# The fifth chunk's output rows transposed as float32r from a copy, and its gating and routing issued two to three products later

## The chip, the cores and the metric

The kernel runs on one core of one Trainium2 chip. A time is the device time of one execution in microseconds. The kernel before takes 934.78 us (median of three runs, 934.42 to 935.09).

## The reference

Three stages follow each other. A linear attention over 4 batches, 8 heads, 576 positions and 64 channels gives 2304 rows of 512. A dense layer takes the elementwise maximum of three products and multiplies it with a fourth matrix. A mixture of 8 experts sends every row to the two experts with the largest noisy gate values.

```python
x = attn_out.transpose(0, 2, 1, 3).reshape(B * S, H * D)          # 2304 x 512
h = np.maximum(np.maximum(x @ w1, x @ w2), x @ w3)                # 2304 x 768
x = h @ w_out                                                     # 2304 x 512
logits = x @ w_gate
noise_scale = np.log1p(np.exp(x @ w_noise))
noisy_logits = logits + noise_scale * noise                       # 2304 x 8
top2 = np.argpartition(-noisy_logits, 2, axis=1)[:, :2]
top2_w = softmax of the two chosen values
for e in range(8):                                                # hidden width 1024
    out[rows of e] += top2_w * (np.maximum(x[rows] @ e_w1[e], 0) @ e_w2[e])
```

## The kernel before, in words

Every large product is made of three TensorE products of float32r operands: each operand is split into a high part and the rest, and high times high, high times rest and rest times high are summed in PSUM.

The dense layer works on six chunks of 384 rows (`NCHUNK` is 6, a chunk is three tiles of 128 rows; in the code they are counted from 0, so the fifth chunk is 4 and the last is 5). For a chunk, `first` (L899) is called for six blocks `f` of the hidden width and three weights `j`, 18 times; one call is 12 matmuls and is called a product here, numbered 0 to 17 in a chunk. After the three products of a block, `larger` (L909 on VectorE, L907 on ScalarE), `hidden_high` (L916) and `hidden_low` (L920) make the block's hidden operand, and `second` (L930, 9 matmuls) adds it to the chunk's output in three PSUM banks. The last `second` of a chunk is issued behind product 0 of the next chunk, and `finish` then copies the three output tiles out: `x2_out` (L937 on ScalarE) into the tile `x2`, and a DMA on SP's queue (L942) into the table `x2d` in HBM.

What follows for a chunk `c - 1` is laid between the products of chunk `c`, in four pieces of `tail`: piece 0 transposes two of the three output tiles on TensorE (`x2_turn`, 8 transposes), piece 1 the third (4 transposes), piece 2 computes the gate values (`gates`, L970), piece 3 turns them back to rows (`gates_turn`, L982) and starts the generator `route` by `route_at`. `TAILS` says behind which products the pieces stand: the first tuple for chunks 1 to 4, the second for the last chunk, in which the fifth chunk's rows are handled. For chunks below `PLAIN` the transposes read a second tile, `x2r`, of type float32r, which a DMA on SP's queue (L947) copies from `x2`; there are two such tiles for three copies. For the others the transposes read `x2` as plain float32 (L957).

`route` is a chain of some thirty small instructions on VectorE, with ScalarE and TensorE in between: from the gate values (`lg`, L1003) to the list of slots (`si`, L1073). GpSimd then issues six indirect DMAs (L1077, one per tile and choice), which write each row's number and weight into the table `meta` in HBM, sorted by expert.

The mixture then runs its experts in turn. Expert 0 begins with up to 512 rows (`cap_a`) of the first five chunks; what the last chunk sends to it is handled later as a unit of its own. For it, GpSimd's queue holds, behind the six scatters of the fifth chunk, one DMA that reads the list of rows back from `meta` (`load_meta`, L1106, tile `emeta`) and four indirect DMAs that gather those rows from `x2d` (`gather_x`, L1139, tile `gx`). TensorE transposes the gathered rows (`turn_x`, L1149) behind product 17 of the last chunk: two tiles, then a `second`, then two tiles, then the last `second`. Then come expert 0's products (L1263).

The order on TensorE, ScalarE, VectorE and SP's queue is written out beforehand. Each call is put on a plan at a planned time (`pe` adds a duration to a running clock, `after` adds an offset to it), and the calls are issued in the order of these times. So a change of `TAILS` also shifts the planned times of what is tied to the clock behind it, and the places of those instructions in all four orders. GpSimd's instructions stand in the order in which they are issued.

Between the products stand two more kinds of work. `sum_job` loads quarters of later experts' first weights (L1402, SP), adds them on GpSimd (L1410 to L1415), splits them (L1419 on ScalarE, L1424 on VectorE) and stores both parts (L1426, SP, 512 KB each). In the last chunk `refill` loads expert 0's weights (L1384 and L1381, SP) and splits them (L1434 on ScalarE into `wh`, L1442 on VectorE into `wl`).

Of the kernel before, what the change touches and what calls it, by code (L numbers as in the profile page):

```python
# [38 lines left out]
def tile_linear_attention__then__moe__then__noisy_top2_moe(  # L39
# [37 lines left out]
    NCHUNK = NT // CT  # L77
# [852 lines left out]
                nc.tensor.matmul(st["acc", c][t], a[:, ts_], b_, start=(f == 0 and n == 0),  # L930
                                 stop=(f == F1 - 1 and n == 2))

    PLAIN = NCHUNK - 2

    def x2_out(c, t):
        x2 = pools["m2"].tile([P, DM], F32, name="x2", tag="x2", bufs=3)
# [7 lines left out]
    def x2_copy(c, t):  # L944
        if c < PLAIN:
            x2, st["x2", t] = st["x2", t], pools["m3"].tile([P, DM], F32R, name="x2r", bufs=2)
            dq.dma_start(st["x2", t].bitcast(F32), x2)  # L947

    def x2_turn(c, t):
        x2 = st.pop(("x2", t))  # L950
        pt = bank_t()
        for d in range(KD):
            ds_ = slice(d * P, (d + 1) * P)
            if c < PLAIN:
                nc.tensor.transpose(pt[:, ds_].bitcast(F32R), x2[:, ds_], exact)
# [659 lines left out]
            pe(0.35, gates_turn, c)  # L1615
            route_at(c, clock[0])

    TAILS = (4, 6, 7, 8), (1, 2, 3, 4)
    split_at = [0.0, 0.0]

    pairs = [(e, j) for e in range(E)
# [54 lines left out]
    for c in range(NCHUNK):  # L1676
        if c == NCHUNK - 1:
            split_at.append(clock[0] + 25.0)
        for f in range(F1):
            for j in range(3):  # L1680
# [7 lines left out]

                tails = TAILS[c == NCHUNK - 1]
                if c and 3 * f + j in tails:  # L1690
# [241 lines left out]
```

## Time and profile before

| | before |
|---|---|
| median of 3 runs | 934.78 us (934.42 to 935.09) |
| the profiled execution | 935.69 us |
| its span, first to last instruction | 934.1 us |
| PE busy | 924.6 us (99%) |
| DVE / ACT / POOL busy | 616.9 / 491.6 / 540.7 us |
| mean granted clock of TensorE | 0.998 of full speed |

PE is TensorE's matmul stream, PEld its weight loads, DVE VectorE, ACT ScalarE, POOL GpSimd, SP the SyncE queue that issues most DMAs (SPq, POOLq: instructions that only issue or wait). In a line of the timeline the first number is the start in us from the span's start, the second the duration, then engine, line of the code, operation, the tile written, the tiles read, shapes, and in brackets the idle time before it with what ended it. Consecutive like instructions are merged into one line with their count (x8). Matmuls overlap in the pipeline, so the distance from one start to the next is what one costs.

### The profile page before, as it was taken

To read this page: it belongs to the slowest core of one execution; us is meant where nothing else is said; L and a number is where in the kernel's file an instruction comes from. 1 tells how busy PE (TensorE), PEld (TensorE's weight loads), DVE (VectorE), ACT (ScalarE), POOL (GpSimd) and SP (SyncE) were. 2 spreads that over 40 slices of the span, in tenths; PEclk is the share of its full clock that TensorE was granted. 3 is DMA by queue.
4 is the path that set the end of the run, shared out by engine and by line. 5 is a ranking of instruction groups with operands and counts; after the bars stand their busy time and mean duration, and the time that the engine had idled before them with its cause. 6 is when DMAs were issued, how large, how long until landed. Compare 5 with 4: busy or idle time off the path is not lost. (4 is left out here: it accounts for less than half of the span.)

```text
span 934.1 us, 18533 instructions
## 1 busy us (share of the span) xinstructions
PE 924.6 (99%) x6817; PEld 805.1 (86%) x6817; DVE 616.9 (66%) x1292; ACT 491.6 (53%) x1056; POOL 540.7 (58%) x598
## 2 busy tenths in 40 slices
PE   9999999999999999999999999999999999999997
PEld 7677777799999999999997889798898989898895
DVE  6999999997563737364564367667576767567641
ACT  7999999554333334343445147355463635455340
POOL 6788898645554645646443546465574746455362
PEclk9999999999999999999999999999999999999999
DMA  7676663544757575857575367666575856748212
GB/s 195 171 220 170 185 192 104 193 154 138 227 178 251 181 239 178 248 170 216 164 218 204 91 224 248 242 215 233 174 254 175 285 166 204 264 155 296 94 34 73
DMA packets 131101, 178.07 MB, mean 191 GB/s; under 512 B 35998, under 2 KB 90398, under 8 KB 131010
## 3 DMA queue, kind: packets, MB, share of 16 engines
q1 hardware_dynamic: 119522, 146.94, 49.5%
q0 software_dynamic: 10928, 29.62, 9.5%
q8 instruction: 54, 0.88, 0.4%
q10 hardware_dynamic: 560, 0.33, 0.1%
q14 instruction: 37, 0.30, 0.1%
HBM read 123.05 MB, written 51.24 MB: 187 GB/s over the span
## 5 line engine op out<-in xcount | busy, mean ns | idle before, releaser
L899 PE MATMUL s<-xh,wh 128*128 128x384 f32 x432 | 147.3, 341 | 0.0
L899 PE MATMUL s<-xh,wl 128*128 128x384 f32 x432 | 145.2, 336 | 0.0
L899 PE MATMUL s<-xl,wh 128*128 128x384 f32 x432 | 145.1, 336 | 0.0
L1364 POOL DMA_INDIRECT out_dram<-o,emeta x40 | 47.7, 1191 | 97.6 <-DVE o L1362 30.1
L909 DVE TENSOR_TENSOR a<-s,a 128x384 f32<-128x384 f32 x72 | 40.0, 555 | 88.4 <-PE s L899 87.3
L899 PEld LDWEIGHTS s<-xh,wh 128*128 128x128 f32 x432 | 81.1, 188 | 5.4 <-DVE a L909 2.5
L1354 PE MATMUL p<-wh,hh 128*128 128x512 f32 (+1 forms) x208 | 82.9, 399 | 0.0
L1354 PE MATMUL p<-wh,hl 128*128 128x512 f32 (+1 forms) x208 | 82.5, 396 | 0.2 <-POOL hl L1251 0.2
L899 PEld LDWEIGHTS s<-xl,wh 128*128 128x128 f32 x432 | 81.1, 188 | 1.4
L1354 PE MATMUL p<-wl,hh 128*128 128x512 f32 (+1 forms) x208 | 82.1, 395 | 0.0
L899 PEld LDWEIGHTS s<-xh,wl 128*128 128x128 f32 x432 | 81.1, 188 | 0.0
L1442 DVE TENSOR_TENSOR wl<-raw,wh 128x1024 fp32r<-128x1024 f32 x57 | 69.3, 1221 | 14.8 <-ACT wh L1434 13.8
L1213 PE MATMUL s<-gx,wh 128*128 128x304 f32 x336 | 72.5, 302 | 0.0
L1410 POOL TENSOR_TENSOR raw<-raw 128x256 f32<-128x256 f32 x28 | 24.5, 876 | 74.9 <-DMA raw<-in_moe_w_dram 63.4
L132 DVE TENSOR_TENSOR gx<-t,gx 128x512 fp32r<-128x512 f32 (+3 forms) x88 | 41.0, 480 | 35.7 <-ACT gx L131 32.8
L1434 ACT ACTIVATE wh<-raw 128x1024 fp32r<-128x1024 f32 x57 | 58.9, 1053 | 9.4 <-DMA raw<-in_moe_w_dram 9.4
L245 POOL TENSOR_TENSOR nm<-nm,bits 128x512 int32<-128x512 int32 (+1 forms) x32 | 38.2, 1205 | 40.9 <-DVE nm L235 16.1
L916 ACT ACTIVATE hh<-a 128x384 fp32r<-128x384 f32 x36 | 18.8, 523 | 81.1 <-DVE a L909 76.9
L131 ACT ACTIVATE gx<-t 128x512 fp32r<-128x512 f32 (+3 forms) x88 | 36.5, 437 | 39.3 <-DVE t L1188 30.5
L1213 PEld LDWEIGHTS s<-gx,wh 128*128 128x128 f32 x336 | 55.6, 189 | 0.7
L1077 POOL DMA_INDIRECT meta<-mt,si x36 | 38.8, 1077 | 29.7 <-DVE si L1073 20.5
L1213 PE MATMUL s<-gx,wl 128*128 128x304 f32 x168 | 50.9, 303 | 0.0
(323 smaller groups left out, 2635.0 us busy)
## 6 DMA issues: line engine op xcount, KB each, us to landing
raw<-in_moe_w_dram SPq DMA_DIRECT2D x57, 512.0 KB
raw<-in_moe_w_dram SPq DMA_DIRECT2D x56, 256.0 KB
sums<-qh SPq DMA_DIRECT2D x28, 512.0 KB
sums<-raw SPq DMA_DIRECT2D x28, 512.0 KB
wh<-sums SPq DMA_DIRECT2D x28, 512.0 KB
wl<-sums SPq DMA_DIRECT2D x28, 512.0 KB
bits<-in_moe_w_dram SPq DMA_DIRECT2D x18, 512.0 KB
out_dram<-zrow SPq DMA_DIRECT2D x9, 512.0 KB
```

The costliest lines, as they stand in the source:

```text
L131: nc.scalar.activation(hi, src, AF.Copy)
L132: nc.vector.tensor_tensor(lo, src, hi.bitcast(F32), op=ALU.subtract)
L245: in_order(nc.gpsimd.tensor_tensor(m_[:, i:i + w], m_[:, i:i + w], low[:, i:i + w], op=ALU.add))
L899: nc.tensor.matmul(p_, a[:, d, fs], b_, start=(n == 0), stop=(n == 3 * KD - 1))
L909: nc.vector.tensor_tensor(a, p_, st.pop("a"), op=ALU.max)
L1077: ins = nc.gpsimd.indirect_dma_start(out=meta, out_offset=bass.IndirectOffsetOnAxis(ap=si[:, t, kk:kk + 1], axis=0), in_=mt[:, t, kk, :], ...
L1213: nc.tensor.matmul(bk["p"], a[:, d, fs], b_[:, d, :], start=(d == 0 and i == 0), stop=(d == 1 and i == 2))
L1354: nc.tensor.matmul(p_, a, b_[:, fw], start=(f == 0 and r == 0), stop=(f == (3 if seven(n) else F2 - 1) and r == 2))
L1364: alone(e, nc.gpsimd.indirect_dma_start(out=out, out_offset=bass.IndirectOffsetOnAxis(ap=mt[:m, i, 1:2], axis=0), in_=o[:m], in_offset=Non ...
L1410: ins = nc.gpsimd.tensor_tensor(a22, a21, a22, op=ALU.add)
L1434: nc.scalar.activation(WE[e, i][0], st["w2", e, i], AF.Copy)
L1442: nc.vector.tensor_tensor(wl, st.pop(("w2", e, i)), wh.bitcast(F32), op=ALU.subtract)
```

## The change

`PLAIN` goes from 4 to 5: the fifth chunk's three output tiles are copied into `x2r` by DMA as well, and its 12 transposes become float32r. In the last chunk the four pieces of the fifth chunk's tail move from behind products 1, 2, 3, 4 to behind products 3, 5, 6, 7.

```diff
-    PLAIN = NCHUNK - 2
+    PLAIN = NCHUNK - 1
...
-    TAILS = (4, 6, 7, 8), (1, 2, 3, 4)
+    TAILS = (4, 6, 7, 8), (3, 5, 6, 7)
```

On TensorE's queue, this is where the last chunk's first `second` into its own banks (`p_` with a number, L930) stands before the change: the whole gating is already behind it.

```order
L899 MATMUL s_6164<-xl,wh 128x384
L899 MATMUL s_6164<-xh,wl 128x384
L930 MATMUL p_6181<-wh,hh 128x512
L930 MATMUL p_6181<-wl,hh 128x512
L930 MATMUL p_6181<-wh,hl 128x512
```

And this is the same `second` after the change, on the same queue:

```order
L899 MATMUL s_6147<-xl,wh 128x384
L899 MATMUL s_6147<-xh,wl 128x384
L955 MATMUL t_6166<-exact,x2r 128x128 x4
L930 MATMUL p_6174<-wh,hh 128x512
L930 MATMUL p_6174<-wl,hh 128x512
L930 MATMUL p_6174<-wh,hl 128x512
```

The third tile's transposes (L955, from the copy `x2r`) now stand right ahead of it, and the gates and `gates_turn` come behind it and one and two products on.

On VectorE, in the fifth chunk's route, between the count of the experts' rows (`run`, L1047) and the weights (`den`, L1061), with the rows taken out and put in:

```order
-L1045 TENSOR_TENSOR r_6240<-ohs 128x8
-L1046 TENSOR_TENSOR r_6240<-r_6240,ohs 128x8
-L1047 TENSOR_TENSOR run_96<-r_6240,run_95 128x8
+L1045 TENSOR_TENSOR r_6317<-ohs 128x8
+L1046 TENSOR_TENSOR r_6317<-r_6317,ohs 128x8
+L1047 TENSOR_TENSOR run_96<-r_6317,run_95 128x8
+L1442 TENSOR_TENSOR wl<-raw,wh 128x1024
 L1061 TENSOR_SCALAR den<-ex 128x3
 L1062 RECIPROCAL mt<-den 128x3
 L1063 TENSOR_TENSOR mt<-ex,mt 128x3
```

The first weight split of the refills (L1442), which stood behind the route, now stands within it.

On SP's queue, after the change, the copies stand among the stores of the output tiles, and the third behind two stores of a sum job:

```order
+L947 DMA x2r<-x_6059 128x512
+L942 DMA x2d<-x_6059 128x512
+L947 DMA x2r<-x_6064 128x512
+L942 DMA x2d<-x_6064 128x512
+L942 DMA x2d<-x_6069 128x512
+L1402 DMA raw<-in_moe_w_dram 128x2x256 x2
+L1426 DMA sums<-qh 128x4x256
+L1426 DMA sums<-raw 128x4x256
+L947 DMA x2r<-x_6069 128x512
```

Three issues (L947) are added; the order of the others around them is as it was, but for one pair of quarter loads (L1402) further ahead, which now stands in front of a sum job's two stores.

## Rows read from the trace of the kernel before

**Rows 1.** The page's first part: busy time, share of the span and count by engine
```profile
PE 924.6 (99%) x6817; PEld 805.1 (86%) x6817; DVE 616.9 (66%) x1292; ACT 491.6 (53%) x1056; POOL 540.7 (58%) x598
```
**Rows 2.** Timeline of POOL: scatters of the fifth chunk, list read back, first gather
```profile
461.67 1.01 POOL L1077 DMA_INDIRECT meta<-mt,si  x1 [11.32 <-DVE si L1073]
...
468.97 0.96 POOL L1077 DMA_INDIRECT meta<-mt,si  x1 [0.30 <-issue]
475.90 0.82 POOL L1106 DMA_DIRECT2D emeta<-meta  x1 [5.96 <-DMA meta<-mt,si]
479.67 1.01 POOL L1139 DMA_INDIRECT gx<-x2d,emeta  x1 [2.95 <-DMA emeta<-meta]
```
**Rows 3.** DMA traffic of 479 to 485 us: POOL's queue, packets, MB, share
```profile
q0 software_dynamic: 160, 0.52, 23.9%
```
**Rows 4.** DMA traffic of 479 to 490 us: busy tenths in 40 slices of 0.275 us
```profile
DMA  1079996946998999975649999999986532000000
```
**Rows 5.** Timeline of PE: the transposes of the gathered rows, a second between them
```profile
487.03 0.81 PE L1149 MATMUL t<-exact,gx 128*128 128x128 f32 x8
487.68 0.47 PE L930 MATMUL p<-wh,hh 128*128 128x512 f32 x1
...
489.84 0.80 PE L1149 MATMUL t<-exact,gx 128*128 128x128 f32 x8
```
**Rows 6.** Timeline of PE: fourth chunk's float32r transposes; starts of two products in a row
```profile
394.96 0.80 PE L955 MATMUL t<-exact,x2r 128*128 128x128 f32 x8
395.59 0.41 PE L899 MATMUL s<-xh,wh 128*128 128x384 f32 x1
...
427.22 0.34 PE L899 MATMUL s<-xh,wh 128*128 128x384 f32 x1
...
429.30 0.34 PE L899 MATMUL s<-xh,wh 128*128 128x384 f32 x1
```
**Rows 7.** Timeline of PE: fifth chunk's plain transposes, and its gates_turn
```profile
441.87 1.03 PE L957 MATMUL t<-ident,x 128*128 128x128 f32 x8
442.66 0.42 PE L899 MATMUL s<-xh,wh 128*128 128x384 f32 x1
...
444.83 0.60 PE L957 MATMUL t<-ident,x 128*128 128x128 f32 x4
...
450.45 0.74 PE L982 MATMUL t<-fold,gT 128*128 128x16 f32 x6
```
**Rows 8.** Timeline of SP: two stores and the fourth chunk's third copy; a later store
```profile
394.41 0.38 SPq L1426 DMA_DIRECT2D sums<-raw  x1
395.44 0.50 SPq L947 DMA_DIRECT2D x2r<-x  x1
...
448.97 0.38 SPq L1426 DMA_DIRECT2D sums<-raw  x1
```
**Rows 9.** DMA traffic of 395 to 399 us: busy tenths in slices of 0.1 us
```profile
DMA  9999999999999999999999999995000000000000
```
**Rows 10.** Timeline of DVE: the route's weights, and the first weight split behind it
```profile
459.96 0.16 DVE L1061 TENSOR_SCALAR den<-ex 128x3 f32<-128x3 f32 x1
...
467.71 1.25 DVE L1442 TENSOR_TENSOR wl<-raw,wh 128x1024 fp32r<-128x1024 f32 x1 [2.41 <-ACT wh L1434]
```
**Rows 11.** Timeline of ACT: behind that route's last step, and the first split's high part
```profile
458.84 0.47 ACT L907 ACTIVATE a<-s 128x384 f32<-128x384 f32 x1
...
466.63 1.05 ACT L1434 ACTIVATE wh<-raw 128x1024 fp32r<-128x1024 f32 x1
```
**Rows 12.** Timeline of POOL: list read back and first gather behind the last chunk's scatters
```profile
520.29 1.39 POOL L1106 DMA_DIRECT2D emeta<-meta  x2 [2.26 <-DMA meta<-mt,si]
523.41 1.03 POOL L1139 DMA_INDIRECT xg<-x2d,emeta  x1 [1.20 <-DMA emeta<-meta]
```
**Rows 13.** Stages at the end: us, busy by engine (PE first), PEclk, DMA share, GB/s
```profile
927.00:928.00 1.00, 0.81 (x4) 0.28 (x2) 0.15 (x1) 0.00 (x0) 0.00 (x0) 1.00 0.00 0
...
931.00:932.00 1.00, 0.00 (x0) 0.00 (x0) 0.00 (x0) 0.00 (x0) 0.00 (x0) 0.62 0.04 12
```

## The prediction

> **What bounds the kernel now.** The page's first part comes first: TensorE is busy for 924.6 of the span's 934.1 us, every other engine for two thirds or less [rows 1]. So the end moves by what TensorE gains or loses, and the question is whether a wait can grow long enough to hold it. I then read GpSimd's timeline around the fifth chunk, because the change moves what feeds it. The chain is plain there [rows 2]: the first scatter starts at 461.67, released by `si`; the sixth starts at 468.97; the list is read back at 475.90, after 5.96 us of waiting for the scatters to land; the first gather of expert 0's rows starts at 479.67. None of these steps can be passed, since they share one queue and each needs the one before.
>
> How much room is there behind it? The traffic of 479 to 485 us holds 0.52 MB of GpSimd's queue [rows 3], which is two gathered tiles of 256 KB: the first pair has landed by 485, at most 5.3 us after the first gather's start. In the longer window DMA is busy in 34 slices of 0.275 us [rows 4], so all four tiles have landed by 488.4, which is 8.7 us after that start. TensorE takes the first pair at 487.03 and the second at 489.84 [rows 5]. The room is about 2.0 us for the first pair and 1.4 us for the second. Whatever delays `si` by more than that is paid by TensorE.
>
> **What the change does, part by part.**
>
> *The transposes.* Eight plain ones keep the next product away for 442.66 - 441.87 = 0.79 us [rows 7], eight float32r ones for 395.59 - 394.96 = 0.63 us [rows 6]. That saves 0.16 us, for the third tile's four half as much, together 0.24 us, all on TensorE.
>
> The Trainium skill's page "FP8 and Floating Point Precision", section "TensorE Precision Notes", says that true FP32 takes four passes through the array. By that the twelve transposes would shrink to a quarter, and some 0.9 us would be gained, as an estimate. The rows above show a fifth off, not three quarters, and the measured price goes into the sum.
>
> *The order on TensorE.* `gates_turn` stood behind product 4 and now stands behind product 7, and the last chunk's first `second` now comes ahead of it. A product takes 429.30 - 427.22 = 2.08 us [rows 6], a `second` 489.84 - 487.68 = 2.16 us [rows 5]. So `gates_turn` comes 3 x 2.08 + 2.16 - 0.24 = 8.2 us later. By itself that costs TensorE nothing: it only swaps the order of its own work.
>
> *The third copy.* It is issued when its turn comes on SP's queue, behind two stores of a sum job. In the fourth chunk it was issued 1.03 us after the second of these stores [rows 8], and the traffic ended at 397.9 [rows 9], 2.5 us after the issue. The corresponding store stood at 448.97 [rows 8], 4.1 us behind the end of product 2 at 444.83 [rows 7]; now product 2 ends at 441.87 + 2.08 = 443.95, so the store goes at about 448.1, the copy at 449.1, and it has landed at 451.6. TensorE asks for it at 443.95 + 3 x 2.08 + 0.63 = 450.8, plus about 0.1 for the slow first matmul behind the eight transposes. I take a wait of 0.7 us; nothing if the stores go sooner, 2 us if the extra traffic of the first two copies (256 KB each) still stands in front. The first two copies have two products more and cost nothing. What stands on SP behind them, quarter loads and stores, is not needed before the later experts, and that cover is tens of microseconds.
>
> *The route on VectorE.* It starts 8.2 + 0.7 = 8.9 us later. In it, one instruction is new: L1442 stands ahead of `den`, and waits for ScalarE's L1434. Without it `den` would come at 459.96 + 8.9 = 468.9 [rows 10]. ScalarE's L907 behind the route's last step comes at 458.84 + 8.9 = 467.7, L1434 0.4 us later at 468.1 [rows 11]; L1442 starts 467.71 - 466.63 = 1.1 us behind it and takes 1.25 us [rows 10, 11], so `den` comes at 470.4. That is 1.5 us more, on the path; zero if the split can run earlier. Behind `den` only `si`, and behind that GpSimd, which have nothing else to do meanwhile.
>
> *GpSimd's chain.* All together 10.4 us later: first scatter at 472.1, the sixth 7.3 us on at 479.4, done at 480.4. The wait for their landing was 5.96 us with the refills in flight [rows 2] and 2.26 us in a quiet stretch [rows 12], so the list is read back between 482.6 and 486.3. From there to the first gather it was 3.8 us [rows 2] or 3.1 us [rows 12]: 485.7 to 490.1. I take the middle, 487.9, since the refill loads are still running when the scatters land, but dry up once TensorE stands.
>
> The Trainium skill's page "DMA: Bandwidth & Descriptors", section "Anatomy of one DMA — SWDGE (gpsimd) path", gives about 2.0 us of fixed cost for a DMA of this queue, most of it the receipt of the write. By that the list would be read back at the early end, and the shift would be near 5 us, as an estimate. The quiet stretch's 2.26 us agrees, the 5.96 us of the place in question does not; this stands as a rival.
>
> *What TensorE then waits for.* The first pair lands at 487.9 + 5.3 = 493.2 (491.0 to 495.4). TensorE is there at 487.03 - 0.24 + 0.7 = 487.5 and stands for 5.7 us (3.5 to 7.9). The second pair lands at 487.9 + 8.7 = 496.6 (494.4 to 498.8). With the clock at full the `second` between the pairs is done 2.8 us behind the first pair's start, at 496.0, and the second pair's transposes would start at 496.6, 6.8 us later than before.
>
> *The clock.* At the end of the span TensorE's last matmul ends at 927.8, and in 931 to 932 the granted clock is down to 0.62 on average, on its way from 2.4 to 1.2 GHz [rows 13], with the engine idle all that time. A stand of 5.7 us should bring the clock down too. At the half level the 2.8 us between the pairs take up to 5.6, to 498.8. No row shows how soon the clock comes back; I take two thirds of the loss, 1.9 us, and the second pair at 497.9.
>
> **The sum.** 497.9 - 489.84 = 8.1 us on TensorE. Everything behind it hangs on TensorE's order and moves along, and since TensorE was already without gaps, nothing later gives it back. On the profiled execution's 935.69 us that is 943.8. That execution lies 0.9 us above the median of the runs, 934.78; on the median it is 942.9 us.
>
> **The rivals.**
>
> *A shorter chain.* The scatters land in the quiet time, the clock stays up, and the split costs less. With the early ends above, the second pair is taken at 494.4, a shift of 4.6 us: 939.4 us. For it speaks that the refills stop when TensorE stands; against it, that the loads were dense when the scatters landed before.
>
> *A longer chain.* The third copy costs 2 us and the scatters wait in full: first pair at 495.4 + 1.3, with the whole clock loss 502, 12 us: 947 us. For it speaks the extra traffic; against it, that both must come together.
>
> *Not slower.* The mechanism is a chain that shrinks to its floor: no wait for the copy, no split within the route (2.2 us off), the quiet landing and the quiet read-back. Then the first gather starts at 483.5, and if the gathers also land 1.5 us sooner than before, because nothing else runs, the second pair is there at 490.7, 0.9 us later than before: 935.5 us, no change. It decides only if all five hold; the read-back is what shows it, at 480.4 or before. Below this lies only the 0.24 us of the transposes: 934.5 us, if the wait on the scatters were not needed for these rows. The bracket at the read-back says it is [rows 2].
>
> **How the numbers follow.** My forecast, a shift of 6.3 to 10 us, has 0.62; the shorter chain 0.20; the longer 0.09; not slower 0.09 in all. A measurement of this kernel tells 0.2% from no change, which is 1.9 us; of the last case I give 0.07 to no change and 0.02 to faster. So slower has 0.91. The range reaches down into the shorter chain and up to the part of the longer one that one mishap gives: 938.8 to 946.0 us. The likeliest case by itself spans 941.1 to 944.8.
>
> **What would show it.** In the changed kernel's trace: `gates_turn` near 459; a wait of under 2 us ahead of the third tile's transposes; L1442 between `run` and `den`; the first scatter near 472, the list read back at 482 to 486; TensorE idle ahead of the first L1149 for 3.5 to 8 us, with the gathers as releaser, and a stretch of clock below 1.00 behind it. The prediction is wrong if the first gather starts before 483, if TensorE's idle time ahead of L1149 is under 2 us, or if the experts' stage behind it is shorter than before by some microseconds.

## The result, and the profile after

| | before | after |
|---|---|---|
| median | 934.60 us (933.15 to 935.09, 6 runs) | 943.98 us (942.69 to 946.80, 6 runs) |
| profiled execution / its span | 935.69 / 934.1 us | 944.93 / 943.4 us |
| mean granted clock | 0.998 | 0.994 |

The ratio is 1.0105, 95% interval 1.0095 to 1.0115: slower by some 9.4 us, where 8.1 us were forecast.

The page's first part, as in [rows 1]:

```profile
PE 926.6 (98%) x6817; PEld 806.3 (85%) x6817; DVE 614.9 (65%) x1292; ACT 491.2 (52%) x1056; POOL 540.1 (57%) x598
```

TensorE's busy time grew by 2.0 us only, its span by 9.3; so most of the loss is time in which it stands. TensorE's longest waits (what it waits for: us in total, times, longest):

```profile
PE t L1149 <- DMA gx<-x2d,emeta: 6.5, 3, 4.6
PE t L955 <- DMA x2r<-x: 1.8, 1, 1.8
```

Before, neither place had a wait; of the three at L1149 the last, 1.08 us at 601.28, is a later one that has its like of 0.89 us before. TensorE's timeline, for [rows 5] and [rows 7]:

```profile
445.64 0.81 PE L955 MATMUL t<-exact,x2r 128*128 128x128 f32 x8
...
452.54 0.51 PE L955 MATMUL t<-exact,x2r 128*128 128x128 f32 x4 [1.83 <-DMA x2r<-x]
...
460.23 0.74 PE L982 MATMUL t<-fold,gT 128*128 128x16 f32 x6
...
493.24 0.72 PE L1149 MATMUL t<-exact,gx 128*128 128x128 f32 x4 [4.63 <-DMA gx<-x2d,emeta]
494.71 0.72 PE L1149 MATMUL t<-exact,gx 128*128 128x128 f32 x4 [0.75 <-DMA gx<-x2d,emeta]
495.23 0.76 PE L930 MATMUL p<-wh,hh 128*128 128x512 f32 x1
...
499.19 0.83 PE L1149 MATMUL t<-exact,gx 128*128 128x128 f32 x8
```

`gates_turn` comes 460.23 - 450.45 = 9.78 us later. The first eight transposes of gathered rows, one group before, are two groups of four with a wait ahead of each, and the `second` behind them takes 499.19 - 495.23 = 3.96 us instead of 2.16 [rows 5].

The route between (VectorE), for [rows 10]:

```profile
469.65 0.17 DVE L1047 TENSOR_TENSOR run<-r,run 128x8 bf16<-128x8 f32 x1
470.08 1.23 DVE L1442 TENSOR_TENSOR wl<-raw,wh 128x1024 fp32r<-128x1024 f32 x1 [0.26 <-ACT wh L1434]
471.22 0.16 DVE L1061 TENSOR_SCALAR den<-ex 128x3 f32<-128x3 f32 x1
```

And GpSimd's chain, for [rows 2]:

```profile
472.92 1.00 POOL L1077 DMA_INDIRECT meta<-mt,si  x1 [21.93 <-DVE si L1073]
...
480.34 0.96 POOL L1077 DMA_INDIRECT meta<-mt,si  x1 [0.30 <-issue]
486.50 0.82 POOL L1106 DMA_DIRECT2D emeta<-meta  x1 [5.20 <-DMA meta<-mt,si]
489.66 1.01 POOL L1139 DMA_INDIRECT gx<-x2d,emeta  x1 [2.33 <-DMA emeta<-meta]
```

`den` is 11.26 us later, the first scatter 11.25, the read-back 10.60, the first gather 9.99. The first gathered tile is transposed only 6.21 us later: before, it had lain ready until 487.03, 7.36 us behind the gather's start; now TensorE takes it the moment it lands, 3.58 us behind that start.

The clock beside it (windows of 1 us: busy time by engine, PE first, then the granted clock, DMA share, GB/s):

```profile
491.00:492.00 1.00, 0.00 (x0) 0.00 (x0) 0.00 (x0) 0.00 (x0) 0.92 (x1) 1.00 0.58 106
492.00:493.00 1.00, 0.00 (x0) 0.00 (x0) 0.00 (x0) 0.00 (x0) 0.78 (x1) 0.71 0.61 193
...
498.00:499.00 1.00, 1.00 (x4) 0.80 (x3) 0.00 (x0) 0.00 (x0) 0.11 (x1) 0.50 0.00 0
499.00:500.00 1.00, 1.00 (x10) 0.80 (x9) 0.00 (x0) 0.28 (x1) 0.00 (x0) 0.87 0.00 0
```

It falls from 2.4 to 1.2 GHz (1.00 to 0.50) within the stand and is back only at the second pair of tiles. From that pair's start to the end of the span it is 444.2 us, before 444.3: nothing behind it loses or gains. So the whole loss, 499.19 - 489.84 = 9.35 us, is there when the second pair starts. On TensorE it is made of four parts: 1.58 us by which it comes later to the first tile (488.61 against 487.03, the copy's wait of 1.83 us less the cheaper transposes), 4.63 us of standing there, 1.34 us more from the first tile to the `second` (1.99 against 0.65), and 1.80 us more for the `second`. The experiments take them apart.

### The profile page after: what moved, and what is told of

It reads as the page before. It is cut to its first block, busy times and chain, and to the rows that moved or that the text cites. A ratio compares the mean times of both kernels' runs of the same rounds, so it can differ in the third digit from the quotient of the medians.

```text
span 943.4 us, 18540 instructions
## 1 busy us (share of the span) xinstructions
PE 926.6 (98%) x6817; PEld 806.3 (85%) x6817; DVE 614.9 (65%) x1292; ACT 491.2 (52%) x1056; POOL 540.1 (57%) x598
## 5 line engine op out<-in xcount | busy, mean ns | idle before, releaser
L1442 DVE TENSOR_TENSOR wl<-raw,wh 128x1024 fp32r<-128x1024 f32 x57 | 69.0, 1218 | 8.2 <-ACT wh L1434 5.8
L1362 DVE SCALAR_TENSOR_TENSOR o<-p,emeta,pv 128x512 f32<-128x512 f32 (+1 forms) x26 | 19.5, 749 | 49.9 <-PE p L1354 43.3
```

The lines of the kernel that those rows point to most:

```text
L1442: nc.vector.tensor_tensor(wl, st.pop(("w2", e, i)), wh.bitcast(F32), op=ALU.subtract)
```

## The experiments

Times are medians of runs made beside runs of the kernel before (934.45 to 934.76 us), ratios to these with their 95% interval. The trace columns are starts in the profiled execution: `gates_turn`, the last scatter, the read-back with the wait for the scatters' landing in front of it, the first tile of gathered rows on TensorE with its wait, and the second pair.

| kernel | us | ratio | gates_turn | last scatter | read-back (wait) | first tile (wait) | second pair |
|---|---|---|---|---|---|---|---|
| before | 934.60 | 1 | 450.45 | 468.97 | 475.90 (5.96) | 487.03 (0) | 489.84 |
| e3_one_later | 934.82 | 0.9993 to 1.0013 | 451.86 | 469.37 | 475.88 (5.54) | 486.33 (0) | 489.14 |
| e2_copy_only | 938.21 | 1.0026 to 1.0051 | 454.08 | 472.61 | 480.19 (6.62) | 490.66 (0) | 493.60 |
| e7_two_later | 941.59 | 1.0056 to 1.0090 | 456.08 | 475.58 | 481.75 (5.20) | 490.05 (3.07) | 495.92 |
| e1_move_only | 942.38 | 1.0060 to 1.0093 | 458.78 | 479.08 | 485.78 (5.75) | 492.51 (5.35) | 497.81 |
| e11_three_later | 942.28 | 1.0063 to 1.0097 | 461.31 | 480.54 | 483.83 (2.21) | 491.69 (4.12) | 497.59 |
| after | 943.98 | 1.0095 to 1.0115 | 460.23 | 480.34 | 486.50 (5.20) | 493.24 (4.63) | 499.19 |
| e4_copy_first | 941.94 | 1.0066 to 1.0099 | 458.57 | 478.82 | 483.00 (3.23) | 491.40 (4.46) | 496.73 |
| e5_clock_kept | 942.86 | 1.0068 to 1.0102 | 460.26 | 480.62 | 486.98 (5.40) | 493.73 (1.06) | 497.71 |
| e6_split_behind | 945.39 | 1.0096 to 1.0141 | 460.06 | 479.03 | 485.85 (5.68) | 492.62 (4.18) | 498.50 |
| e8_second_ahead | 943.63 | 1.0086 to 1.0128 | 459.76 | 479.90 | 485.69 (4.84) | 492.63 (2.40) | none |
| e9_copy_split_clock | 939.90 | 1.0037 to 1.0070 | 457.92 | 476.99 | 484.23 (6.02) | 491.42 (2.09) | 494.81 |
| e10_small_refills | 938.06 | 1.0027 to 1.0047 | 460.02 | 479.72 | 482.12 (1.44) | 488.77 (0.38) | 492.74 |
| e12_before_small_refills | 934.29 | 0.9987 to 1.0005 | 450.19 | 468.70 | 471.99 (2.33) | 486.76 (0) | 489.57 |

**The two halves apart.** The kernel before with the new places alone, and with the copies alone.

```diff
e1:  -    TAILS = (4, 6, 7, 8), (1, 2, 3, 4)
e1:  +    TAILS = (4, 6, 7, 8), (3, 5, 6, 7)
e2:  -    PLAIN = NCHUNK - 2
e2:  +    PLAIN = NCHUNK - 1
```

> Half of the change: the tail's pieces behind products 3, 5, 6, 7, the fifth chunk's transposes still plain, no copies. Theory (the loss is the later route, and behind it the gathers of expert 0): gates_turn 8.4 us later, the weight split still within the route for 1.5 us, first scatter near 471.6, TensorE stands some 5 us ahead of the gathered rows' transposes and then runs at the half clock; second pair near 498, total 7 to 8.5 us slower than before (942 to 943). Rival (the copies, their traffic and the wait for them are the loss): 0 to 2 us slower (934.6 to 936.6).

> The other half: copies and float32r transposes, but the pieces behind products 1, 2, 3, 4 as before. Theory: TensorE waits for the copies at the transposes (1 to 2 us at the first two tiles, 1 to 4 us at the third), and the route starts later by the same waits, so the room ahead of the gathers stays what it was: no new wait at the gathered rows, the granted clock stays at 1.00, 2 to 6 us slower (936.6 to 940.6). Rival (the copies are nearly free and the float32r transposes gain): within 1 us of before.

The places alone cost 7.7 us, most of the loss. The copies alone cost 3.5 us, at another place and in another way, as TensorE's timeline of e2_copy_only shows:

```profile
443.25 0.51 PE L955 MATMUL t<-exact,x2r 128*128 128x128 f32 x4 [1.48 <-DMA x2r<-x]
444.52 0.50 PE L955 MATMUL t<-exact,x2r 128*128 128x128 f32 x4 [0.76 <-DMA x2r<-x]
...
448.29 0.67 PE L955 MATMUL t<-exact,x2r 128*128 128x128 f32 x4
...
454.08 0.74 PE L982 MATMUL t<-fold,gT 128*128 128x16 f32 x6
```

At the old places the first two copies are asked for too soon: 2.24 us of waiting. I expected the clock to stay; it did not (e2's windows):

```profile
444.00:445.00 1.00, 0.48 (x5) 0.51 (x6) 0.00 (x0) 0.40 (x1) 0.92 (x2) 1.00 0.69 262
445.00:446.00 1.00, 1.00 (x6) 1.00 (x6) 0.00 (x0) 0.60 (x1) 0.74 (x2) 0.74 0.85 302
446.00:447.00 1.00, 1.00 (x4) 1.00 (x4) 0.00 (x0) 0.00 (x0) 0.00 (x0) 0.50 0.92 280
```

The rest of `gates_turn`'s 3.63 us is that. The gathers still have their room there: no wait at L1149. So the later places serve the copies, and the copies alone are no way to the gain of the cheaper transposes.

In e2 the profile names a weight load (`raw`), and not the scatters, as what ended the 6.62 us ahead of the read-back:

```profile
480.19 0.82 POOL L1106 DMA_DIRECT2D emeta<-meta  x1 [6.62 <-DMA raw<-in_moe_w_dram]
```

**How the loss grows with the places.** Plain transposes, the pieces behind products 2 to 5 (e3), 3 to 6 (e7), and 4, 6, 7, 8 (e11); e1 stands between the last two.

```diff
e3:   +    TAILS = (4, 6, 7, 8), (2, 3, 4, 5)
e7:   +    TAILS = (4, 6, 7, 8), (3, 4, 5, 6)
e11:  +    TAILS = (4, 6, 7, 8), (4, 6, 7, 8)
```

> Plain transposes, all four pieces one product later (behind 2, 3, 4, 5). Theory: si comes 2.1 us later, of which the room of 1.4 to 2.0 us ahead of the gathered rows takes most: 0 to 1 us slower (934.6 to 935.6), first wait of up to 1 us at the gathered rows' transposes. Rival (no room, every delay is paid): 2.1 us slower (936.7).

> Plain transposes, the pieces behind products 3, 4, 5, 6: two products and one second later, 6.3 us. [...] Rival (a smooth loss in proportion to the later place, 8.4 us of delay for 9.3 us): 7 us.

> The kernel before, with its plain transposes, and the tails of the fifth chunk put at products 4, 6, 7 and 8 (before 1, 3, 4 and 5 counted from the same place less one; e3 one, e7 two product places later, e1 on the changed kernel's places). Theory (the room ahead of the gathers holds the first product, and from there on each further product's delay of some 2.1 us is a product's delay of the end): the last gating product at about 460.9, first gather's first tile about 494.5, total 944 to 945, 2.1 us above e1's 942.4. Rival (the loss is one step, paid once when the stand appears and the clock falls, and the rest is absorbed): total 941.5 to 943, as e1 and e7.

One product later (e3) is free, as the room of [rows 4, 5] says: in its trace the first gather starts 0.2 us later than before and TensorE is at the gathered rows 0.7 us sooner, so some 0.9 us of the room is used up. In e7 the gates come two products and a `second` later, since that `second` now stands ahead of them, and it costs 6.9 us: the stand appears, and with it the clock's price (from the `second` between the pairs to the second pair it takes 3.96 us, as in the changed kernel). In e7 the quarter split L1424 stood within the route (`den` at 466.79, 6.8 us later than before with `gates_turn` 5.6 later). But e11 went against the theory: `gates_turn` 2.5 us behind e1's, the same time. GpSimd's timeline of e11 shows what took it up:

```profile
480.54 1.09 POOL L1077 DMA_INDIRECT meta<-mt,si  x1 [0.30 <-issue]
483.83 0.82 POOL L1106 DMA_DIRECT2D emeta<-meta  x1 [2.21 <-DMA meta<-mt,si]
488.15 1.01 POOL L1139 DMA_INDIRECT gx<-x2d,emeta  x1 [3.50 <-DMA emeta<-meta]
```

Its last scatter is 1.5 us behind e1's (479.08), yet has landed 2.0 us sooner: the wait is 2.21 us instead of 5.75. So the price of the route's last link isn't fixed; what it depends on was the next question.

**What makes the scatters land late.** The changed kernel (e10) and the kernel before (e12) with the eight refill loads of expert 0 cut to 64 columns; expert 0's weights are left out of what they compute.

```diff
+            if key == 0:
+                dq.dma_start(raw[:, :64], e_w2[e, f * 2 * P:f * 2 * P + P, :64])
+            else:
                 dq.dma_start(raw..., e_w2[ds(e, 1), f * 2 * P:(f + 1) * 2 * P, :]...)
+        elif first_ == KD and key == 0:
+            dq.dma_start(raw[:, :64], e_w1[e, i * P:(i + 1) * P, :64])
```

> The changed kernel with the eight refill loads of expert 0's weights, which are under way in the route, cut to 64 columns each (the splits read those columns again and again, so expert 0's weights are left out of what is computed). Theory (the 5.2 us in which POOL waits for the six scatters to land, against 2.26 us in the quiet round later, is made longer by those loads on the same DMA engines): landing wait 2.3 to 3.5 us, read-back about 483.5 to 485, first gather's first tile at 490.5 to 492, total 941 to 942.5. Rival (the wait is a fixed cost of the first landing, or comes of other traffic such as the stores): landing wait 4.8 to 5.6 us, first tile 493 to 493.6, total as the changed kernel, 942.7 to 945.

> The kernel before with the refill loads of expert 0 cut to 64 columns each, as e10 has them (expert 0's weights are left out of what is computed). The question is whether e10's 5.9 us against the changed kernel came out of the route, or whether fewer bytes make any kernel faster. Theory (the loads make the landing wait longer in both orders, but in the order before the gathered rows have room, so that nothing waits for the earlier landing): landing wait about 1.5 us instead of 5.96, gather 0 at about 474.5 to 476 instead of 479.67, first tile of the first gather at 486.5 to 487.5 as before without a wait, total 933.5 to 935.5, ratio 0.999 to 1.001. Rival (the loads cost their bytes in later stages too): total 929 to 932.5, ratio below 0.998.

GpSimd's timeline of e10:

```profile
479.72 0.96 POOL L1077 DMA_INDIRECT meta<-mt,si  x1 [0.30 <-issue]
482.12 0.82 POOL L1106 DMA_DIRECT2D emeta<-meta  x1 [1.44 <-DMA meta<-mt,si]
485.21 1.14 POOL L1139 DMA_INDIRECT gx<-x2d,emeta  x1 [2.27 <-ACT a L907]
```

The wait fell from 5.20 to 1.44 us, the stand ahead of the first tile from 4.63 to 0.38, the clock stayed up, and the time fell by 5.9 us, more than either theory said. DMA's share of time in 470 to 475 us went from 0.89 to 0.08:

```profile
470.00:475.00 5.00, 5.00 (x27) 4.59 (x27) 4.42 (x12) 1.11 (x2) 1.77 (x2) 1.00 0.89 304
```
```profile
470.00:475.00 5.00, 5.00 (x27) 4.59 (x26) 4.31 (x12) 1.54 (x3) 1.96 (x2) 1.00 0.08 17
```

(the changed kernel above, e10 below). In the kernel before the same cut makes the wait 2.33 us instead of 5.96 and brings the gathers 4.6 us sooner (e12):

```profile
471.99 0.82 POOL L1106 DMA_DIRECT2D emeta<-meta  x1 [2.33 <-DMA meta<-mt,si]
475.11 1.01 POOL L1139 DMA_INDIRECT gx<-x2d,emeta  x1 [2.30 <-ACT a L907]
```

and the time is the same. (For the gathers of e10 and e12 the profile names ScalarE's L907 as what ended the wait; the list's landing fits it as well, 2.3 us behind its issue in e10 by the profile's DMA view.) So the loads do hold the scatters up, in both orders; before, the room hid it, after, TensorE pays for it. The same view gives the median time of the six scatters from issue to landing: 2.6 us in e10 and 3.4 in e12, but 4.6 to 6.1 us in the six runs with the loads for which it has one (e4, e5, e6, e8, e9, e11). The 2.9 us that e10 still loses at the second pair are the copy's wait (1.62 us) and two short ones at the first pair (0.38 and 0.95 us). The Trainium skill's page "DMA: Bandwidth & Descriptors", section "Anatomy of one DMA — SWDGE (gpsimd) path", gives about 2.0 us of fixed cost for a DMA of this queue. The 1.44 and 2.33 us without the loads are near it, the 5 to 6 us of most runs with them are not.

**The third copy.** Its two stores in front are planned later, so that the copy goes first.

```diff
-                    sum_job(1.8 if f in (3, 4) else 0.65)
+                    sum_job(1.8 if f in (3, 4) else 2.9 if c == NCHUNK - 1 and f == 0 else 0.65)
```

> The changed kernel, with the sum job of the last chunk's first block put 2.2 us later in the plan, so that the third copy is issued ahead of its two stores and not behind them. Theory: the wait of 1.8 us ahead of the third tile's transposes goes (0 to 0.4 left), gates_turn and the whole chain come 1.5 to 1.8 us sooner, the stand ahead of the gathered rows stays as long: 1.5 to 1.8 us faster than the changed kernel. Rival (the scatters wait for the refill loads anyway, so the chain ends at the same time): the same time as the changed kernel, the stand longer by 1.8 us.

The wait at L955 is gone (450.90, no bracket). `gates_turn` comes 1.66 us sooner, the last scatter 1.52, and the time is 2.0 us below the changed kernel's; the two intervals just overlap. The landing wait fell to 3.23 us as well, but the read of the list behind it took 4.00 us instead of 2.33, so this link gave part back.

**The clock.** 72 matmuls of no use ahead of the four transposes.

```diff
+            nc.tensor.matmul(t[:, :P], ones, ones, start=True, stop=True)     # 72 times
```

> The changed kernel, with 72 dummy matmuls (bf16, 128 columns, some 4 us in all, written to a bank that nothing reads) on TensorE ahead of the gathered rows' transposes. Theory: the granted clock stays at 1.00, the second between the two pairs takes 2.2 us and not 4.0, the second pair has landed by 496.7 and starts at 497.3 and not at 499.2: 1.5 to 2.0 us faster than the changed kernel. Rival (the stand itself is all of it, the second pair lands late anyway): under 0.4 us.

TensorE's timeline of e5:

```profile
493.73 0.51 PE L1149 MATMUL t<-exact,gx 128*128 128x128 f32 x4 [1.06 <-DMA gx<-x2d,emeta]
495.20 0.51 PE L1149 MATMUL t<-exact,gx 128*128 128x128 f32 x4 [0.96 <-DMA gx<-x2d,emeta]
...
497.71 0.80 PE L1149 MATMUL t<-exact,gx 128*128 128x128 f32 x8
```

The granted clock is 1.00 in every window there, and from the first tile to the second pair it takes 3.98 us instead of 5.95: 2.0 us are the clock's share. What is left over the 2.81 us of before, 1.2 us, is the wait for the second tile. The time fell by 1.1 us only: the gathers came 0.6 us later in this run, and the two kernels' intervals overlap.

**The split in the route.** L1442 behind `si`.

```diff
-            at(t, w2_low, en, j)
+            at(t + (1.5 if (en, j) == pairs[0] else 0.0), w2_low, en, j)
```

> The changed kernel, with one instruction moved: the first weight split on VectorE (L1442) behind si and not ahead of den. Theory: den and si come 1.5 us sooner, first scatter at 471.4, the stand shorter by about that: 1.2 to 1.6 us faster than the changed kernel. Rival (the read-back is set by the refill loads' traffic and not by si): under 0.4 us.

`den` came 1.66 us sooner (469.56), the last scatter 1.31, and then the landing wait grew from 5.20 to 5.68 us; 0.7 us reached TensorE in the trace, and none the median (945.39 us, 943.21 to 946.74). Whether it is worth something by itself this run does not tell.

**The second tile's wait.** The `second` goes ahead of all four tiles, so that the stand is filled with it.

```diff
+    pe(G2, second, c, F1 - 2)          # ahead of the four turn_x, no longer between them
```

> The changed kernel, with the last but one second of the dense layer ahead of all four transposes of gathered rows instead of between the pairs. Theory (TensorE has nothing to do in the stand, so any work put into it is free): the stand shrinks from 4.6 to some 2.5 us, the last transposes come when their rows land (496.7), 1 to 2 us faster than the changed kernel. Rival (the loss sits in what follows, the experts' stage): the same time.

The first wait fell to 2.40 us, but three more followed (TensorE's timeline of e8):

```profile
492.63 0.51 PE L1149 MATMUL t<-exact,gx 128*128 128x128 f32 x4 [2.40 <-DMA gx<-x2d,emeta]
494.25 0.72 PE L1149 MATMUL t<-exact,gx 128*128 128x128 f32 x4 [1.10 <-DMA gx<-x2d,emeta]
495.54 0.72 PE L1149 MATMUL t<-exact,gx 128*128 128x128 f32 x4 [0.56 <-DMA gx<-x2d,emeta]
496.63 0.72 PE L1149 MATMUL t<-exact,gx 128*128 128x128 f32 x4 [0.37 <-DMA gx<-x2d,emeta]
```

and the clock fell all the same (0.51 to 0.72 us for four). The span shrank by 2.2 us; the medians, 943.63 and 943.98, can't be told apart.

**Three terms at once.** e4's and e6's edits, and 54 matmuls as in e5.

> The changed kernel with three of its costs taken back at once: the third copy of the fifth chunk goes ahead of the last chunk's stores on SP (so its 1.8 us wait at L955 should go, as it did in e4), the weight split L1442 stands behind the route on VectorE (den 1.5 us sooner, as in e6), and 54 matmuls of no use ahead of the four transposes of the first gather keep the granted clock at 1.00 (as in e5). Theory (the route is one chain from the last gating product to the first gather, and each of the three is a term of it): first scatter about 469.7 to 470.3, first tile of the first gather about 490 to 491, second gather's first tile about 494 to 495.5, total 938 to 940, some 4 us under the changed kernel. Rival (what is saved ahead of the scatters is given back in the wait for their landing, as half of it was in e6): landing wait grows to 5.5 us or more, first tile at 492 or later, total 941.5 to 943.

939.90 us: 4.1 us of the 9.4 are back. In the traces the second pair moves by 4.38 us, and by 2.46, 1.48 and 0.69 us, together 4.63, in the three runs apart; so, in one trace each, the terms nearly add up. Both sides of the expectation saw something: the time came as the theory had it, and the landing wait grew to 6.02 us as the rival had it, the scatters being 3.4 us sooner.

No run beat the kernel before. What the change can gain is at most the 0.24 us of the transposes, less than a measurement tells.

## Why the prediction was right

The outcome (943.98 us against 942.9, in the range of 938.8 to 946.0) came by the mechanism named. Step by step:

- *Place of the loss.* One stand ahead of L1149 with the gathers as releaser, one of under 2 us at L955, and nothing given back behind them: all three are in the trace.
- *Order.* 8.2 us forecast. 9.78 us less the 1.83 of the copy's wait is 7.95, and e1, with plain transposes, has 458.78 - 450.45 = 8.33.
- *Third copy.* 0.7 us forecast, 0 to 2 allowed; 1.83 measured, and in e4, with the two stores behind the copy, it is gone. The copy was issued sooner than I had it (447.58 against 449.1), since the stores went sooner, but TensorE could start on its tile only 5.0 us behind that (452.54), where I had read 2.5 us from the fourth chunk's. In the fourth chunk the traffic was over at once [rows 9]; here most of it is over at 450.6, and a rest of 14 to 41 GB/s runs on to 452.1. Why stays open.
- *Split in the route.* 1.5 us forecast; `den` is 11.26 - 9.78 = 1.48 us further back. e6 shows the size (1.66 us), but not that it reaches the time.
- *GpSimd's chain.* Read-back forecast at 482.6 to 486.3, came at 486.50, 0.2 us outside; first gather at 485.7 to 490.1, came at 489.66, 1.8 us behind the middle that I took. Of that 0.8 us is the later first scatter (472.92 against 472.1), the rest the landing, at the late end, less the read-back, at the early one (3.16 us). My reason for the middle, that the loads dry up, was the weak one: TensorE stands only from 488.6 on, when the scatters have landed and the list is being read back. e10 and e12 show that it is the loads that make this wait long.
- *First pair.* 493.2 forecast, first tile at 493.24: that they agree so closely is luck, two differences against each other. The gather was 1.8 us late, and its tile landed 3.6 us behind it instead of the 5.3 that I had as a bound for both tiles. TensorE came at 488.6 instead of 487.5 because of the copy.
- *The mis-sized term.* I let both tiles of the first pair be there at 493.2, so that the `second` would start at 493.85. The second tile's transposes start 1.47 us behind the first's, and the `second` at 495.23: 1.4 us later, which is the 1.3 us by which the second pair (499.19 against 497.9) missed the forecast. The landing of the second pair, by which I set it in turn, decided nothing: no wait stands there, and the gathers' traffic ends at 496.7 (the changed kernel's DMA busy tenths from 488 to 500 us, in slices of 0.3):

```profile
DMA  4000000000093675776594579876200000000000
```

- *Clock.* 1.9 us forecast; the `second` alone takes 3.96 - 2.16 = 1.80 us more, and e5 gets 2.0 us back. The size was right, its reason was not: I took two thirds of the loss because the clock might come back on the way. It stayed at 0.50 in every window from 493 to 499 us, through the whole `second`, whose nine matmuls took 1.83 times as long as before, not twice.

The rivals: the shorter chain needed a landing in quiet; e10, which makes it quiet, comes to 938.06 us, near the 939.4 that I had given it. The longer chain had the copy at 2 us, which nearly came, but no full wait of 5.96 us with it. The 2.8 us between the pairs did more than double (5.95 us), but by the clock only in part: 2.0 us are its share (e5), the rest is the second tile's wait. "Not slower" needed five things at once: the quiet read-back (3.16 us from it to the first gather) and the earlier landing of the gathers (7.0 us behind the first instead of 8.7) held, the three in front of them did not, and the read-back at 486.50 instead of 480.4 says so.

## What to carry to other kernels

A chain that is hidden by a few microseconds of room costs nothing until the room is used up, and then all at once: one product later was free, two products and a `second` cost 6.9 us. By then the delay was past the room, a weight split had slid into the chain too, and the stand on the bounding engine brought its clock down. So before a step is moved to save a part of a microsecond on the bounding engine, read how much room its consumers have, from the landing of the last transfer to its use. And small scattered writes at the end of such a chain are priced by the traffic beside them: look at what loads run in that stretch before taking a wait from a quiet one.

## What the runs showed of the hardware that I had not expected

- The same six scatters and the same read-back waited between 1.44 and 2.33 us without the refill loads (e10, e12) and between 2.21 and 6.02 us with them (e11, e9), leaving out e2, where the profile names a weight load as what ended the 6.62 us. Where in the second range it falls isn't monotonic in the start: last scatters at 480.34 and 480.54 waited 5.20 and 2.21 us. What decides it there stays open.
- The granted clock stayed at 1.00 after the single stand of 1.83 us at L955 in the changed kernel, but fell to 0.50 after the stands of 1.48 and 0.76 us in e2, which have one tile's transposes between them.
- Single executions spread more than the effects of some edits: the changed kernel's six over 4.1 us, and fifteen of the kernel before, run beside e12, over 3.2 (933.89 to 937.12). So differences of 1 us between the variants are not told by these medians. What the text says of them rests on the waits within one trace each, and that is one execution.
